# A two-layer recurrent-memory transformer: half-height weight loads and row-paired transposes in the prologue

## The chip, the core and the metric

The kernel runs on one core of a Trainium2 chip. The metric is device time in microseconds for one execution, as the median of several runs. One further execution is profiled; every number of an instruction, an engine or a transfer comes from that one.

## What is computed

Two kinds of layer alternate, twice each, on 2048 tokens of 448 numbers in bf16. The first kind is attention in segments of 32 tokens with a memory of 8 rows that each segment hands to the next, so that the segments of a layer form one chain of 64 steps. The second is a gated feed-forward layer (448 to 1792 and back).

```python
def _A_ref(x, mem0, Wq, Wk, Wv, Wo, seg_len):      # H = 16 heads of Dh = 256
    ...
    for s in range(n_seg):
        xs = x[:, s * seg_len:(s + 1) * seg_len, :].copy()
        h = jnp.concatenate([mem, xs], axis=1)
        q = jnp.einsum('btd,dhe->bhte', h, Wq)
        k = jnp.einsum('btd,dhe->bhte', h, Wk)
        v = jnp.einsum('btd,dhe->bhte', h, Wv)
        scores = jnp.einsum('bhqe,bhke->bhqk', q, k) * scale
        scores = jnp.where(mask[None, None], scores, -1000000000.0)
        p = _softmax(scores, axis=-1)
        o = jnp.einsum('bhqk,bhke->bhqe', p, v)
        o = jnp.einsum('bhte,hed->btd', o, Wo)
        mem = o[:, :M, :].copy()
        outs.append(o[:, M:, :])
    return jnp.concatenate(outs, axis=1)

def _B_ref(x, W_gate, W_up, W_down):
    ...
    h = gate * up                                  # gate with its negative part set to zero
    return jnp.einsum('bsf,fd->bsd', h, W_down)

x = x + _A_ref(_layernorm(x), mem0, Wq, Wk, Wv, Wo, seg_len)
x = x + _B_ref(_layernorm(x), W_gate, W_up, W_down)
x = x + _A_ref(_layernorm(x), mem0, Wq, Wk, Wv, Wo, seg_len)
x = x + _B_ref(_layernorm(x), W_gate, W_up, W_down)
```

## The kernel before

**Two stages.** The kernel does not compute q, k and v. In a prologue it fuses, head by head, Wq with the transpose of Wk into `A_sb` (with `A3`, `A3z` for the last 64 of the 448 dimensions), and Wv with Wo into `B_sb`. The main loop (`step`, from line 830) then takes segment after segment through `A_sb`, the softmax and `B_sb`, with the feed-forward layer (`Feed`) woven in. Both attention layers run in the same steps, the second four steps behind the first. The change is in the prologue alone (lines 100 to 343).

**The prologue's passes.** Two heads are 512 columns of a weight matrix, and 448 rows of it are seven chunks of 64 (`NPASS` = 7). A pass takes one tile `nat` of 128 partitions by 7 by 512, which holds 512 columns of two matrices. There are 12 passes: eight of Wq with Wk (p = 0 to 7), then four of Wv for p and p + 1.

- `load_two` (line 210) loads a pass with four transfers on SP's queue: for each matrix one of 384 rows over all 128 partitions (384 KB) and one of the last 64 rows (64 KB), put into the row half `ROWS[r]` of the middle chunk. `nat` has four buffers. `load_outs` (line 219) loads 512 rows of Wo, 448 KB, after the Wv passes have begun.
- `transposed` (line 230) turns a pass round: four banks of PSUM, `tpw`, one for each 128 of the 512 columns (e), with seven 128 by 128 transposes each, and four copies of 896 elements into `two`, one by ScalarE (ACT) and three by VectorE (DVE). In pass 0 (`first`) the transposes of the first three chunks come before the others, and the copies are shared two and two.
- `fuse_qk` (line 250) multiplies: for three groups of 128 dimensions (kd) and the two heads (eo) products of 384 and of 64 columns, then the last 64 dimensions, with copies by ACT and DVE into `A_sb`, `A3` and `A3z`. `fuse_vo` (line 277) and `fuse_vo_last` do the same for Wv and Wo into `B_sb`.

**The order of PE.** All TensorE (PE) instructions go through `mm` and `tr`, which chain each to the one before (`in_order`), so PE's order is the program's. Transposes of pass p + 1 stand ahead of the products of pass p, but for pass 0, whose products come before the transposes of pass 1:

```python
cur = flip_next(0)
for p in range(NP):
    if p:
        nxt = flip_next(p + 1)
    fuse_qk(p, cur)
    cur = nxt if p else flip_next(1)
```

In the Wv half, the transposes of the next pass stand ahead of the products of two p's. Ahead of it all stand 32 transposes of the identity into `warm` (line 313).

**The other engines and the queues.** The order of DVE, ACT, GpSimd (POOL) and the queue of SP is set by a scheduler that puts ready work first. `tc.keep_in_program_order` (also named `queued`) holds an instruction behind the one traced before it on its engine, without a wait. Weight loads are held so, in the order Wq/Wk passes 0 to 7, Wv 0, Wo 0 and 1, Wv 1, Wo 2 and 3, and so on; three passes are issued at the start, and each `flip_next` asks for one more. Eight semaphores serve the transfers in turn, so that a transfer is issued only when the one eight before it has landed.

**Tokens.** Line 100 loads the first 128 tokens into `xp[1]`, first on SP's queue. Their norm (`row_stats`, `normed`) is written after p = 3, and the transposes of its result after the products of p = 4; the two instructions of `normed` are held in program order, the statistics are not. Lines 340 to 343 and 828 load further tokens into row halves of `xa` and `xp`.

**Constants.** POOL makes the identity, clears `hT` and `TQ` (lines 143 and 155) and copies the mask into `hT`; DVE makes the mask and `blk` (lines 128 and 129).

Of the kernel before, what the change touches and what calls it, by code (L numbers as in the profile page):

```python
# [8 lines left out]
BF = mybir.dt.bfloat16  # L9
F32 = mybir.dt.float32  # L10
# [5 lines left out]
DM = 448  # L16
# [13 lines left out]
TB = BLK * SEG  # L30
# [9 lines left out]
NPASS = 7  # L40
ROWS = (slice(0, 64), slice(64, 128))
# [12 lines left out]
def build_kernel(ctx, tc, A_x, A_mem0, A_Wq, A_Wk, A_Wv, A_Wo, B_W_gate, B_W_up, B_W_down, out,  # L54
                 ntiles=16, nseg=64):
    nc = tc.nc
    P = nc.NUM_PARTITIONS
    x_dram = A_x[0]
# [9 lines left out]
    psum = ctx.enter_context(tc.tile_pool(name="psum", bufs=7, space=bass.MemoryType.PSUM))  # L68
# [12 lines left out]
    def mm(*a, **k):  # L81
        in_order(nc.tensor.matmul(*a, **k))  # L82

    def tr(*a):
        in_order(nc.tensor.transpose(*a))  # L85

    def evac(eng, dst, src):
        if eng is nc.scalar:
            nc.scalar.copy(dst, src)  # L89
        else:  # L90
            eng.tensor_copy(dst, src)  # L91


    xa = [glob.tile([P, DM], BF, name=f"xa{i}") for i in range(3)]
    xp = [glob.tile([P, DM], BF, name=f"xp{i}") for i in range(2)]

    def block(i):
        return slice(TB * i, TB * i + TB)

    nc.sync.dma_start(xp[1][:], x_dram[0:128])  # L100

    ident = glob.tile([P, P], BF, name="ident")
    make_identity(nc, ident[:])

# [8 lines left out]
    rowf = glob.tile([P, 3], F32, name="rowf")  # L113
# [8 lines left out]
    for b in range(4):  # L122
        o = 0 if b % 2 == 0 else MEM
        nc.vector.tensor_scalar(out=maskS[:, b, o:o + SEG], in0=keyf[:, b // 2, :], scalar1=rowf[:, 2:3],
                                scalar2=MASKVAL, op0=ALU.is_gt, op1=ALU.mult)

    blk = glob.tile([P, 2], F32, name="blk")
    nc.vector.tensor_copy(blk[:, 1:2], rowf[:, 1:2])
    nc.vector.tensor_scalar(out=blk[:, 0:1], in0=blk[:, 1:2], scalar1=-1.0, scalar2=1.0,
                            op0=ALU.mult, op1=ALU.add)  # L130

    half = glob.tile([P, 1], F32, name="half")
# [7 lines left out]
    hTb = []  # L140
    for i in range(2):
        t = glob.tile([P, BLK, HW], BF, name=f"hT{i}")
        nc.gpsimd.memset(t[:], 0.0)
        for part, q in enumerate(QR):
            for c in range(2):
                nc.gpsimd.tensor_copy(t[q:q + 16, :, 4 * HI + 64 * c:4 * HI + 64 * c + L],
                                      maskS[q:q + 16, 2 * part + c, :].unsqueeze(1).to_broadcast([16, BLK, L]))
        hTb.append(t)
# [3 lines left out]
    TQ = []  # L152
    for hf in range(2):
        t = glob.tile([P, 5, 6, 64], BF, name=f"TQ{hf}")
        nc.gpsimd.memset(t[:], 0.0)
        TQ.append(t)

    def row_stats(t):

        stats = p_ln.tile([P, nc.vector.BN_STATS_DIM], F32, tag="ln_stats")  # L160
        nc.vector.bn_stats(stats[:], t[:])
        mv = p_ln.tile([P, 2], F32, tag="ln_mv")
        nc.vector.bn_aggr(mv[:], stats[:])
        rstd = p_ln.tile([P, 1], F32, tag="ln_rstd")
        nc.gpsimd.tensor_scalar(out=rstd[:], in0=mv[:, 1:2], scalar1=EPS, scalar2=None, op0=ALU.add)
        nc.gpsimd.tensor_tensor(out=rstd[:], in0=rstd[:], in1=half[:], op=ALU.pow)
        return t, mv, rstd

    def normed(stat):

        t, mv, rstd = stat
        xn = p_ln.tile([P, 512], BF, tag="ln_xn", bufs=3)
        for a, b, o in ((0, DM, 0), (384, DM, DM)):
            tc.keep_in_program_order(
                nc.vector.tensor_scalar(out=xn[:, o:o + b - a], in0=t[:, a:b], scalar1=mv[:, 0:1],  # L175
                                        scalar2=rstd[:], op0=ALU.subtract, op1=ALU.mult))
        return xn
# [24 lines left out]
    with tc.tile_pool(name="pre", bufs=3) as pre:  # L202
# [4 lines left out]

        queued = tc.keep_in_program_order

        def load_two(a, b):  # L210
            t = pre.tile([P, NPASS, 512], BF, tag="nat", name="nat", bufs=4)
            for r, (src, p) in enumerate((a, b)):
                cols = slice(512 * p, 512 * (p + 1))
                queued(nc.sync.dma_start(t[:, 4 * r:4 * r + 3, :],
                                         src[0:384, cols].rearrange("(k p) n -> p k n", p=P)))
                queued(nc.sync.dma_start(t[ROWS[r], 3, :], src[384:448, cols]))
            return t

        def load_outs(p):
# [9 lines left out]

        def transposed(nat, first=False):  # L230
            o = pre.tile([P, 4, 2 * DM], BF, tag="two", name="two", bufs=2)
            tp = [psum.tile([P, 2 * DM], BF, tag="ps", name="tpw") for _ in range(4)]
            order = sorted(((0, i, e) if first and i < 3 else (1, e, i), e, i) for e in range(4) for i in range(NPASS))
            for _, e, i in order:
                tr(tp[e][:, i * 128:(i + 1) * 128], nat[:, i, e * 128:(e + 1) * 128], ident[:])
            for e in range(4):
                evac(nc.scalar if (e % 2 if first else e == 1) else nc.vector, o[:, e, :], tp[e][:])
            return o

        def dims(t, r, e, c, n=1):  # L240
            o = 64 * c if r == 0 else DM + 64 * ((c + 1) % NPASS)
            return t[:, e, o:o + 64 * n]

        def halves(dst, lhs, rhs):
# [5 lines left out]
        def fuse_qk(p, qk):  # L250
            hf, p4 = divmod(p, 4)
            mx_ps = psum.tile([P, 4, 128], F32, tag="ps", name="mxw")
            for kd in range(3):
                for eo in range(2):
                    aps = psum.tile([P, 3, 128], F32, tag="ps", name="aps")
                    for t in range(2):
                        e = 2 * eo + t
                        mm(aps[:, :, :], qk[:, e, kd * 128:kd * 128 + 128], dims(qk, 1, e, 0, 6),
                           start=(t == 0), stop=(t == 1))
                    for t in range(2):  # L260
                        e = 2 * eo + t
                        mm(mx_ps[:, kd, eo * 64:eo * 64 + 64], qk[:, e, kd * 128:kd * 128 + 128], dims(qk, 1, e, 6),
                           start=(t == 0), stop=(t == 1))
                    evac(nc.scalar if eo or kd == 2 else nc.vector,
                         A_sb[:, kd, hf, eo * 4 + p4:eo * 4 + p4 + 17:8, :], aps[:])
            aps = psum.tile([P, 3, 128], F32, tag="ps", name="aps")
            halves(aps, lambda eo, e: qk[:, e, 384:448], lambda e: dims(qk, 1, e, 0, 6))
            for eo in range(2):
                for t in range(2):
                    e = 2 * eo + t  # L270
                    mm(mx_ps[ROWS[hf], 3, eo * 64:eo * 64 + 64], qk[:, e, 384:448], dims(qk, 1, e, 6),
                       start=(t == 0), stop=(t == 1), tile_position=(0, 64 * hf))
            evac(nc.scalar, A3[:, hf, p4:p4 + 9:4, :], aps[:])
            evac(nc.vector, A_sb[:, 0:3, hf, 24 + p4, :], mx_ps[:, 0:3])
            evac(nc.scalar, A3z[ROWS[hf], p4, :], mx_ps[ROWS[hf], 3])
# [20 lines left out]

        def load_next():
            if len(nat) < len(loads):
                nat.append(load_two(*loads[len(nat)]))
            if len(nat) > NP and len(wos) < NP:  # L300
                wos.append(load_outs(len(wos)))
                wos.append(load_outs(len(wos)))

        for _ in range(3):
            load_next()

        def flip_next(i):
            load_next()
            return transposed(nat[i], i == 0)

        warm = psum.tile([P, 2 * DM], BF, tag="ps", name="warm")
        for i in range(32):
            tr(warm[:, 0:128], ident[:], ident[:])
        cur = flip_next(0)
        for p in range(NP):
            if p:
                nxt = flip_next(p + 1)
            fuse_qk(p, cur)
            cur = nxt if p else flip_next(1)
            if p == 3:  # L320
                xn0 = normed(row_stats(xp[1]))
            if p == 4:
                tps0 = transpose_tokens(xn0)
                for b in range(2):
                    rows_in(nc.vector, b, 0, tps0[:, :, block(b)])
                mtp = psum.tile([P, 4, MEM], BF, tag="ps", name="mtp")
                for kd in range(4):
                    tr(mtp[:, kd, :], mem0_n[:, kd * 128:(kd + 1) * 128], ident[0:MEM, 0:MEM])
                nc.vector.tensor_copy(mem0T[:], mtp[:])
                set_mem(0, mem0T[:].unsqueeze(2), (0,))  # L330
# [7 lines left out]

    for i in range(min(3, nblk)):
        nc.gpsimd.memset(xa[i][:], 0.0)  # L340
        nc.sync.dma_start(xa[i][TB:P, :], x_dram[block(i)])
    if nblk > 2:
        nc.sync.dma_start(xp[0][0:TB, :], x_dram[block(2)])


    main = ctx.enter_context(tc.tile_pool(name="main", bufs=1))
# [555 lines left out]
```

## Time and profile before

| | us |
|---|---|
| median of 3 runs | 1600.96 |
| the runs | 1599.98 to 1604.62 |
| profiled execution | 1600.11 |
| its span, first to last instruction | 1598.3 |
| prologue: until the main loop's first weight load | 74.8 |
| transposes of the last Wv pass begin | 62.2 |
| a Wq/Wk pass, from one pass's transposes to the next's | 4.54 |

The span is what lies between the first and the last instruction; 1.8 us of the execution lie around it. Engines are named PE (TensorE products), PEld (its weight loads, which overlap the products), DVE, ACT, POOL and SP. A line of the timeline gives start and duration in us, the engine, the source line, the operation, what it writes and reads, and in brackets how long the engine stood idle before it and what released it; lines of `mm`, `tr` and `evac` are those of the helper (82, 85, 89, 91), so that the tile tells the place. In rows by stretch of time, each engine's busy time is followed by its instruction count, then the granted share of PE's clock, the busy share of the 16 DMA engines (which can be over 1 when packets overlap) and the rate in GB/s.

### The profile page before, as it was taken

What the parts mean: (1) busy time and instruction counts of PE and PEld (TensorE: products, weight loads), DVE (VectorE), ACT (ScalarE), POOL (GpSimd) and SP (SyncE); (2) the same over time, 40 slices, a digit from 0 to 9 for tenths busy, and PEclk for the clock granted to TensorE, in tenths of its full rate; (3) what the DMA queues carried; (4) which work ended last, traced back from release to release, by engine and by line L of the source; (5) the groups of instructions that cost most, each with busy time, mean ns of one, the idle gap of its engine ahead of it and who ended that gap; (6) DMA issues with size and microseconds to landing.
All of it is one profiled execution on the core that took longest, in us unless ns stands there. A gap on an engine that the chain in (4) does not pass through costs nothing.

```text
span 1598.3 us, 96401 instructions
## 1 busy us (share of the span) xinstructions
PE 1567.8 (98%) x44356; PEld 1439.8 (90%) x44356; DVE 1142.5 (71%) x3859; ACT 762.9 (48%) x2239; POOL 92.9 (6%) x240
## 2 busy tenths in 40 slices
PE   8989999999999999999999999999999999999997
PEld 7678899999999999999999999999999999999886
DVE  6856777777777777777777777777777777777773
ACT  5634445544444445544444445544444445544432
POOL 2110000000000000000000000000000000000000
PEclk9989999999999999999999999999999999999999
DMA  9530000000000000000000000000000000000000
GB/s 257 147 102 8 9 9 4 10 9 10 10 10 9 10 10 4 10 10 9 10 10 10 10 10 4 10 10 10 10 9 9 10 10 4 10 8 7 7 7 6
DMA packets 29461, 33.01 MB, mean 21 GB/s; under 512 B 3320, under 2 KB 28160, under 8 KB 29056
## 3 DMA queue, kind: packets, MB, share of 16 engines
q1 hardware_dynamic: 28992, 26.85, 6.3%
q8 instruction: 346, 5.67, 1.5%
q14 instruction: 59, 0.48, 0.1%
q0 software_dynamic: 64, 0.01, 0.0%
HBM read 23.18 MB, written 1.84 MB: 16 GB/s over the span
## 4 chain that ended last, share of the span: by engine, by line
PE 89%; DVE 7%; ACT 1%; POOL 1%; issue 1%; DMA 0%; POOLq 0%; ACTq 0%; DVEq 0%
PE prj L82 25%; PE ox L82 25%; PE ups L82 10%; PE dps L82 6%; PE o L82 5%; PE y L82 4%; PE Sx L82 2%; PE Sm L82 2%; PE bps L82 1%; PE tpw L85 1%; DVE xn L175 1%; DVE TQ L91 1%; PE aps L82 1%; PE gps L82 1%; PE tps L85 1%; PE pps L85 1%
## 5 line engine op out<-in xcount | busy, mean ns | idle before, releaser
L82 PEld LDWEIGHTS <-B_sb 128*128 128x128 bf16 (+1 forms) x15456 | 495.0, 103 | 27.7 <-issue 19.9
L82 PE MATMUL prj<-hT,A_sb 128*128 128x80 bf16 (+1 forms) x11424 | 441.7, 200 | 0.4 <-issue 0.4
L82 PEld LDWEIGHTS <-A_sb 128*128 128x128 bf16 x11424 | 411.9, 100 | 8.9 <-issue 0.5
L82 PE MATMUL ox<-Y,B_sb 128*128 128x80 bf16 (+4 forms) x5880 | 223.0, 198 | 1.8 <-DVE Y L636 1.8
L82 PE MATMUL ox<-Z,B_sb 128*128 128x80 bf16 (+2 forms) x5712 | 217.7, 199 | 1.3 <-DVE Z L636 1.3
L89 ACT CAST TQ<-prj 128x480 bf16<-128x480 f32 (+1 forms) x380 | 178.5, 497 | 83.0 <-PE prj L82 58.7
L82 PE MATMUL gps<-xT,Wgu_sb 64*128 64x128 bf16 (+1 forms) x3332 | 191.3, 214 | 0.8 <-issue 0.5
L82 PE MATMUL ups<-xT,Wgu_sb 64*128 64x128 bf16 (+1 forms) x3332 | 191.1, 214 | 1.0 <-DVE xT L416 0.5
L82 PEld LDWEIGHTS <-Wgu_sb 64*128 64x128 bf16 x6664 | 179.4, 95 | 4.8 <-issue 2.5
L91 DVE CAST TQ<-prj 128x480 bf16<-128x480 f32 (+1 forms) x228 | 129.3, 573 | 13.4 <-PE prj L82 11.2
L432 DVE SCALAR_TENSOR_TENSOR hh<-gps,ut 128x256 bf16<-128x256 f32 (+1 forms) x238 | 95.3, 407 | 48.0 <-ACT ut L431 35.3
L431 ACT CAST ut<-ups 128x256 bf16<-128x256 f32 (+1 forms) x238 | 85.4, 359 | 83.4 <-PE gps L82 64.9
L91 DVE CAST Y<-y 64x128 bf16<-64x128 f32 (+2 forms) x256 | 102.2, 420 | 14.4 <-ACT Y L89 4.5
L89 ACT CAST Y<-y 64x128 bf16<-64x128 f32 (+2 forms) x256 | 89.4, 379 | 46.6 <-DVE Y L91 41.5
L91 DVE CAST Z<-y 64x128 bf16<-64x128 f32 (+2 forms) x256 | 99.2, 418 | 12.4 <-ACT Z L89 5.5
L89 ACT COPY hT<-tps 128x256 bf16<-128x256 bf16 x32 | 11.9, 372 | 197.5 <-DVE hT L91 197.5
L563 DVE COPY PT<-pps 128x128 bf16<-128x128 bf16 (+1 forms) x206 | 49.6, 254 | 79.1 <-PE pps L85 77.5
L545 ACT ACTIVATE se<-se 128x80 f32<-128x80 f32 (+1 forms) x270 | 71.4, 298 | 68.0 <-DVE se L544 67.2
L89 ACT CAST TZ<-prj 64x320 bf16<-64x320 f32 (+2 forms) x152 | 56.2, 380 | 98.8 <-DVE TZ L91 94.0
L89 ACT CAST Z<-y 64x128 bf16<-64x128 f32 (+2 forms) x256 | 89.2, 378 | 23.9 <-DVE Z L91 17.4
L82 PEld LDWEIGHTS <-hk 40*128 40x128 bf16 (+1 forms) x1989 | 79.9, 95 | 20.5 <-issue 10.6
L551 DVE TENSOR_REDUCE ssum<-se 128x2 f32<-128x80 f32 (+1 forms) x270 | 70.8, 274 | 35.9 <-ACT se L545 33.6
(128 smaller groups left out, 2254.6 us busy)
## 6 DMA issues: line engine op xcount, KB each, us to landing
wo<-in_A_Wo_dram SPq DMA_DIRECT2D x8, 448.0 KB, 7.6
nat<-in_A_Wq_dram SPq DMA_DIRECT2D x8, 384.0 KB, 5.5
nat<-in_A_Wk_dram SPq DMA_DIRECT2D x8, 384.0 KB, 6.1
nat<-in_A_Wv_dram SPq DMA_DIRECT2D x8, 384.0 KB, 7.6
xa<-in_A_x_dram SPq DMA_DIRECT2D x32, 56.0 KB, 2.4
xa<-xp SPq DMA_DIRECT2D x32, 56.0 KB, 1.9
out_dram<-xa SPq DMA_DIRECT2D x32, 56.0 KB, 2.0
xp<-in_A_x_dram SPq DMA_DIRECT2D x30, 56.0 KB, 2.3
```

The lines of the kernel that those rows point to most:

```text
L82: in_order(nc.tensor.matmul(*a, **k))
L85: in_order(nc.tensor.transpose(*a))
L89: nc.scalar.copy(dst, src)
L91: eng.tensor_copy(dst, src)
L175: nc.vector.tensor_scalar(out=xn[:, o:o + b - a], in0=t[:, a:b], scalar1=mv[:, 0:1], scalar2=rstd[:], op0=ALU.subtract, op1=ALU.mult))
L431: nc.scalar.copy(ut[:, :, n], ups[:, :, n])
L432: nc.vector.scalar_tensor_tensor(out=hh[:, 2 * u:2 * u + 2, n], in0=gps[:, :, n], scalar=0.0, in1=ut[:, :, n], op0=ALU.max, op1=ALU.mult)
L545: nc.scalar.activation(se[:], se[:], AF.Exp, scale=SCALE)
L551: nc.vector.tensor_reduce(ssum[:], se[:], axis=AX.X, op=ALU.add)
L563: nc.vector.tensor_copy(PT[:], pps[:].rearrange("p b q -> p (b q)"))
```

## The change

- **Loads.** A pass is loaded with two transfers of 448 KB instead of four: the matrix of r = 0 goes to partitions 0 to 63 and that of r = 1 to partitions 64 to 127, seven chunks of 64 rows each. In pass 0 each matrix comes in two halves of 256 columns (512 bytes in a row), Wq on SP's queue and Wk on ACT's.
- **Transposes.** Each transposes 64 rows by 128 columns; the two row halves of `nat` go into two banks, one after the other for the same columns. Two banks are filled and copied at a time (e = 0, 1 and then 2, 3). A copy takes one matrix and two e's (896 elements), in pass 0 one e (448 elements, shared by DVE and ACT). `dims` follows the new layout.
- **Products of pass 0** run eo = 0 for all three kd first and then eo = 1; the other passes keep their order.
- **Fillers.** The identity transposes ahead of pass 0 become 24 instead of 32, and ten more stand between the transposes of pass 0 and its products.
- **Tokens.** The first 128 tokens are loaded behind the first three passes; their statistics are held in program order on DVE; the later token loads are held on SP behind all weight loads.
- **POOL and DVE.** `blk` is made by POOL; the clearings of `hT` and `TQ` are held in program order.

```diff
-    nc.sync.dma_start(xp[1][:], x_dram[0:128])
...
-    nc.vector.tensor_copy(blk[:, 1:2], rowf[:, 1:2])
-    nc.vector.tensor_scalar(out=blk[:, 0:1], in0=blk[:, 1:2], scalar1=-1.0, scalar2=1.0,
+    nc.gpsimd.tensor_copy(blk[:, 1:2], rowf[:, 1:2])
+    nc.gpsimd.tensor_scalar(out=blk[:, 0:1], in0=blk[:, 1:2], scalar1=-1.0, scalar2=1.0,
                             op0=ALU.mult, op1=ALU.add)
...
-        nc.gpsimd.memset(t[:], 0.0)
+        tc.keep_in_program_order(nc.gpsimd.memset(t[:], 0.0))
...
-    def row_stats(t):
+    def row_stats(t, pin=False):
...
-        nc.vector.bn_stats(stats[:], t[:])
+        (tc.keep_in_program_order if pin else lambda i: i)(nc.vector.bn_stats(stats[:], t[:]))
...
-        def load_two(a, b):
+        def load_two(a, b, first=False):
             t = pre.tile([P, NPASS, 512], BF, tag="nat", name="nat", bufs=4)
-            for r, (src, p) in enumerate((a, b)):
-                cols = slice(512 * p, 512 * (p + 1))
-                queued(nc.sync.dma_start(t[:, 4 * r:4 * r + 3, :],
-                                         src[0:384, cols].rearrange("(k p) n -> p k n", p=P)))
-                queued(nc.sync.dma_start(t[ROWS[r], 3, :], src[384:448, cols]))
+            n = 256 if first else 512
+            for o in range(0, 512, n):
+                for r, (src, p) in enumerate((a, b)):
+                    eng = nc.scalar if first and r else nc.sync
+                    queued(eng.dma_start(t[ROWS[r], :, o:o + n],
+                                         src[:, 512 * p + o:512 * p + o + n].rearrange("(c p) n -> p c n", p=64)))
             return t
...
             o = pre.tile([P, 4, 2 * DM], BF, tag="two", name="two", bufs=2)
-            tp = [psum.tile([P, 2 * DM], BF, tag="ps", name="tpw") for _ in range(4)]
-            order = sorted(((0, i, e) if first and i < 3 else (1, e, i), e, i) for e in range(4) for i in range(NPASS))
-            for _, e, i in order:
-                tr(tp[e][:, i * 128:(i + 1) * 128], nat[:, i, e * 128:(e + 1) * 128], ident[:])
-            for e in range(4):
-                evac(nc.scalar if (e % 2 if first else e == 1) else nc.vector, o[:, e, :], tp[e][:])
+            for ep in range(2):
+                tp = [psum.tile([P, 2, DM], BF, tag="ps", name="tpw") for _ in range(2)]
+                for k in range(2):
+                    for i in range(NPASS):
+                        for r in range(2):
+                            e = 2 * ep + k
+                            tr(tp[r][:, k, 64 * i:64 * i + 64], nat[ROWS[r], i, e * 128:(e + 1) * 128], ident[ROWS[r], ROWS[r]])
+                for k in range(2) if first else (slice(0, 2),):
+                    for r in range(2):
+                        es = slice(2 * ep + k, 2 * ep + k + 1) if first else slice(2 * ep, 2 * ep + 2)
+                        evac(nc.scalar if r and (first or ep == 0) else nc.vector,
+                             o[:, es, DM * r:DM * r + DM], tp[r][:, k:k + 1, :] if first else tp[r][:])
             return o
...
-            o = 64 * c if r == 0 else DM + 64 * ((c + 1) % NPASS)
+            o = DM * r + 64 * c
...
-            for kd in range(3):
-                for eo in range(2):
+            for kd, eo in [(kd, eo) for eo in range(2) for kd in range(3)] if p == 0 else \
+                    [(kd, eo) for kd in range(3) for eo in range(2)]:
...
-                nat.append(load_two(*loads[len(nat)]))
+                nat.append(load_two(*loads[len(nat)], first=not nat))
...
+        queued(nc.sync.dma_start(xp[1][:], x_dram[0:128]))
...
-        for i in range(32):
-            tr(warm[:, 0:128], ident[:], ident[:])
+        def idle(n):
+            for _ in range(n):
+                tr(warm[:, 0:128], ident[:], ident[:])
+
+        idle(24)
         cur = flip_next(0)
+        idle(10)
...
-                xn0 = normed(row_stats(xp[1]))
+                xn0 = normed(row_stats(xp[1], True))
...
-        nc.sync.dma_start(xa[i][TB:P, :], x_dram[block(i)])
+        tc.keep_in_program_order(nc.sync.dma_start(xa[i][TB:P, :], x_dram[block(i)]))
     if nblk > 2:
-        nc.sync.dma_start(xp[0][0:TB, :], x_dram[block(2)])
+        tc.keep_in_program_order(nc.sync.dma_start(xp[0][0:TB, :], x_dram[block(2)]))
```

More of the change, by code (lines that the diff above doesn't have):

```diff
@@ L154, in build_kernel @@
         t = glob.tile([P, 5, 6, 64], BF, name=f"TQ{hf}")
-        nc.gpsimd.memset(t[:], 0.0)
+        tc.keep_in_program_order(nc.gpsimd.memset(t[:], 0.0))
         TQ.append(t)
-    def row_stats(t):
+    def row_stats(t, pin=False):
         stats = p_ln.tile([P, nc.vector.BN_STATS_DIM], F32, tag="ln_stats")
-        nc.vector.bn_stats(stats[:], t[:])
+        (tc.keep_in_program_order if pin else lambda i: i)(nc.vector.bn_stats(stats[:], t[:]))
         mv = p_ln.tile([P, 2], F32, tag="ln_mv")
@@ L252, in fuse_qk @@
             mx_ps = psum.tile([P, 4, 128], F32, tag="ps", name="mxw")
-            for kd in range(3):
-                for eo in range(2):
[L255 to L265, printed above, removed]
+            for kd, eo in [(kd, eo) for eo in range(2) for kd in range(3)] if p == 0 else \
+                    [(kd, eo) for kd in range(3) for eo in range(2)]:
+                aps = psum.tile([P, 3, 128], F32, tag="ps", name="aps")
+                for t in range(2):
+                    e = 2 * eo + t
+                    mm(aps[:, :, :], qk[:, e, kd * 128:kd * 128 + 128], dims(qk, 1, e, 0, 6),
+                       start=(t == 0), stop=(t == 1))
+                for t in range(2):
+                    e = 2 * eo + t
+                    mm(mx_ps[:, kd, eo * 64:eo * 64 + 64], qk[:, e, kd * 128:kd * 128 + 128], dims(qk, 1, e, 6),
+                       start=(t == 0), stop=(t == 1))
+                evac(nc.scalar if eo or kd == 2 else nc.vector,
+                     A_sb[:, kd, hf, eo * 4 + p4:eo * 4 + p4 + 17:8, :], aps[:])
             aps = psum.tile([P, 3, 128], F32, tag="ps", name="aps")
```

## The prediction

> **What bounds the kernel now.** I read first the page's busy rows and the chain that ended last, then stretches of the first 100 us, then the timeline, because the change touches only the prologue (up to 74.8 us) and the transfers behind it.
>
> ```profile
> span 1598.3 us, 96401 instructions
> PE 1567.8 (98%) x44356; PEld 1439.8 (90%) x44356; DVE 1142.5 (71%) x3859; ACT 762.9 (48%) x2239; POOL 92.9 (6%) x240
> PE 89%; DVE 7%; ACT 1%; POOL 1%; issue 1%; DMA 0%; POOLq 0%; ACTq 0%; DVEq 0%
> ```
>
> PE sets the end almost everywhere; DMA has no share of the chain. In stretches (time, then PE, PEld, DVE, ACT, POOL busy, granted clock, DMA share, GB/s):
>
> ```profile
> 5.00:10.00 5.00, 3.23 (x34) 2.26 (x31) 1.15 (x2) 1.71 (x2) 4.86 (x9) 1.00 0.94 281
> 10.00:15.00 5.00, 3.29 (x42) 2.58 (x43) 2.78 (x6) 2.33 (x6) 2.92 (x7) 1.00 1.12 290
> 15.00:20.00 5.00, 5.00 (x73) 4.12 (x71) 4.08 (x8) 3.43 (x7) 0.00 (x0) 1.00 1.03 260
> 25.00:30.00 5.00, 5.00 (x72) 4.03 (x70) 3.72 (x7) 3.65 (x8) 0.00 (x0) 1.00 0.92 257
> 45.00:50.00 5.00, 5.00 (x67) 3.84 (x65) 3.72 (x8) 3.80 (x8) 0.00 (x0) 1.00 1.09 319
> ```
>
> The reader sees PE waiting only before 15 us and full after it, while the transfers keep ahead. The timeline (start, duration, engine, line) gives the waits and the price of a pass:
>
> ```profile
> 7.59 1.05 PE L85 MATMUL tpw<-ident,nat 128*128 128x128 bf16 x16 [1.31 <-DMA nat<-in_A_Wk_dram]
> 12.20 0.93 DVE L175 TENSOR_SCALAR xn<-xp,mv,rstd 128x448 bf16<-128x448 bf16 x1 [3.02 <-POOL rstd L166]
> 13.63 0.52 PE L82 MATMUL aps<-two 128*64 128x384 bf16 x4 [1.70 <-DVE A_sb L91]
> 24.81 1.57 PEld L85 LDWEIGHTS <-nat 128*128 128x128 bf16 x28
> 25.47 1.88 DVE L91 COPY two<-tpw 128x896 bf16<-128x896 bf16 x3
> 29.35 1.57 PEld L85 LDWEIGHTS <-nat 128*128 128x128 bf16 x28
> 62.19 1.56 PEld L85 LDWEIGHTS <-nat 128*128 128x128 bf16 x28 [0.36 <-issue]
> 74.80 0.21 PEld L82 LDWEIGHTS <-A 64*128 64x128 bf16 x12 [0.36 <-DVE B_sb L91]
> ```
>
> A Wq/Wk pass lasts 29.35 - 24.81 = 4.54 us, 1.57 of it transposes. Pass 0 is late: it waits for Wk until 7.59 and for DVE, which sits behind the token norm (L175), until 13.63; the next transposes begin at 14.18. From the last transposes (62.19) to the main loop (74.80) are 12.6 us.
>
> **The change part by part.**
>
> Row pairs. 28 transposes become 28 pairs of 64-row ones with 64 moving columns. The nearest row is the gate/up product of the same shape, two row halves into two banks:
>
> ```profile
> 137.14 1.28 PEld L82 LDWEIGHTS <-Wgu_sb 64*128 64x128 bf16 x84
> ```
>
> (1.28 - 0.10)/83 = 14.3 ns each, 28.6 ns a pair; 28 pairs are 0.80 us, with the last one's 0.1 us left over some 0.84, against 1.57. That saves 0.73 us in each of 11 passes, 8.0 us of PE. Bounds: nothing saved (no overlap) to 0.77. The copies stay four of 896 elements, three on DVE and one on ACT. Per pass DVE then has 1.88 + 1.01 + 0.56 = 3.45 us and ACT 0.91 + 0.48 + 1.25 + 0.48 + 0.26 = 3.38, in a pass that would last 4.54 - 0.73 = 3.81: tight, but not the bound.
>
> The start. Tokens (112 KB) no longer lead the queue, pass 0 comes in halves on two queues, and bn_stats is held back. Before, all of Wk was in at 7.5 us; less 112 KB at the 281 GB/s of that stretch (0.4) it is 7.1, and up to 6.2 if two queues at once fill the engines as the later stretches (319) do. I take 6.8; the first half some 2.1 us sooner. Packets of 512 bytes appear nowhere in the trace; if they cost as much as the 1 KB ones, pass 0 takes 2.6 us more, if half as much, nothing; the linear guess from the 896-byte packets puts them near half. ACT issues two transfers at about 0.6 us each (SP's rows say 0.37 to 0.59); ACT is idle until 8.24 now, so this costs nothing, and would cost 1.2 us in the first copy without that cover. Second half transposed by 7.5, ten filler transposes 0.6 (54 ns each) to 8.1, the first products with eo = 0 and eo = 1 1.1 us each (0.38 per kd in the rows of pass 1), then 0.5: pass 0 ends near 10.8 instead of 14.18. Gain 3.4.
>
> Token norm at pass 3. bn_stats, bn_aggr (0.63 + 0.18), the POOL pair (0.23 + 0.57 and hand-overs, some 1.0), two norms (0.93 + 0.29): 3.1 us of DVE in order, with the copies of the next pass queued behind. Before it cost PE 1.70. It may cost 0 (hidden where PE waits for transfers anyway) to 2.5 (3.1 less DVE's slack of some 0.4 and a little more). The two blk operations (0.14 + 0.15) go to POOL, which idles until 35.8 in the trace. The memsets held on POOL stand in that order already. The five later x loads move from 16-19 us, where they sit between Wq loads, behind the last Wo load; xa is first read at 129 us, so nothing. SP issues 2 instead of 4 a pass: 1.1 us of SP saved that nothing waits for; but eight transfers outstanding now span four passes instead of two.
>
> Loads on one row half. This is the term that decides. A pass is 2 x 448 KB = 917.5 KB. Three bounds from rows: full-width loads keep 319 to 324 GB/s. Wgu's loads alternate between the halves exactly so. The five x loads of 19 to 21 us, each on one half, three in a row on the same one, are the floor:
>
> ```profile
> 19.00:20.00 1.00, 1.00 (x13) 0.69 (x11) 0.24 (x1) 1.00 (x3) 0.00 (x0) 1.00 0.73 127
> 20.00:21.00 1.00, 1.00 (x21) 0.91 (x18) 0.62 (x2) 0.74 (x3) 0.00 (x0) 1.00 0.60 152
> 79.00:81.00 2.00, 2.00 (x80) 1.88 (x73) 1.27 (x8) 1.51 (x8) 1.90 (x5) 1.00 1.00 253
> 81.00:83.00 2.00, 1.10 (x25) 0.87 (x24) 1.54 (x8) 0.53 (x3) 2.00 (x2) 1.00 1.01 240
> 36.00:55.00 19.00, 19.00 (x215) 13.29 (x212) 14.46 (x26) 13.81 (x29) 0.09 (x1) 1.00 1.10 324
> ```
>
> I take 245 GB/s (Wgu, the nearest shape, DMA share 1.0, so saturated): X = 917.5/245 = 3.74 us a load, ends at 3.06 (300) and 6.1 (151). The last Wv pair lands at 6.8 + 0.4 (tokens behind pass 2) + 11 X + 3 x 2.83 (two Wo per group at 324) = 15.7 + 11 X = 56.8. After it come its transposes, 0.84, and the last four fuse_vo: 12.6 - 1.56 = 11.0, so 11.9 in all. End of prologue 27.6 + 11 X = **68.7**. The path of PE alone is shorter: 10.8 + 0.84 + 7 x 3.81 + 3 x 0.84 + 4 x 5.5 (56.7 to 62.2) = 62.8, or 65.3 with the norm's 2.5. So transfers become the bound, and PE waits some 0.3 us a pass and longer in the Wv groups.
>
> Behind the prologue everything (Wgu loads, POOL's Y and Z memsets) is released by its last products and moves along. Sum: 68.7 - 74.8 = -6.1 us. The profiled execution took 1600.11 us (span 1598.3 and 1.8 around it), so 1594.0; the median of the runs is 0.85 above it: **1594.9 us**.
>
> The clock adds noise: after PE's wait at 82-84 us the granted clock is 0.77 in 80-90 and 0.55 in 90-100. A shift of the prologue may cut or lengthen this; +-2 us.
>
> **The rivals.**
>
> PE sets the pace (22%). If the two halves interleave over the 16 engines as well as full rows do, X = 3.06 and transfers would end at 61.3; PE's 62.8 to 65.3 counts: 1588.1 to 1590.6 on the profiled run, about 1590.2 as a median. For it: pass 0's first Wgu loads ran at 294 GB/s in 77-78. Against: they fall to 240 once the queue is full.
>
> Halves overlap only partly (18%). If the engines stay mostly in step on one half, the rate lies between the x loads' 152 and Wgu's 245, say 199: X = 4.6, end 78.2, +3.4, about 1604. For it: a nat load keeps each engine on a half for 28 packets, Wgu for 4. The Trainium skill, "SBUF — State Buffer", section "Can I just issue two DMAs to hit both halves?", speaks against the change: two transfers on the two halves gained only 6% over one, 196 GB/s in its table; by that, an estimate of 208 GB/s and 4.4 us a load, the time would be about 1602. By that rule the Wgu rows should not exceed it; they show 240 to 253, so the trace agrees only in direction.
>
> In lockstep, slower (10%). All engines on one half at a time, at the x loads' 151 GB/s: X = 6.1, end 94.7, +20, 1621. The sign turns at X = 4.29 (214 GB/s); it is 0.3% slower from 4.73 (194). Against it: the sixteen engines' shares of one Wgu load land over some 2 us, longer than the load itself takes at 245, so they do not march in step.
>
> Pairs don't overlap (5%). Transposes stay 1.57 and PE's path is 62.8 + 8 = 70.8 to 73.3; -1.5 to -4: 1597 to 1599.5. Against it: the gate/up row.
>
> **How the numbers follow.** The forecast has 45%, its own range 1591.5 to 1598.5 (X from 3.44 to 4.05). This kernel's runs differ by 0.3% (4.8 us) without cause, so faster means X under 3.86, 238 GB/s. Faster: 0.22 and two thirds of 0.45, 0.52; same: the rest of the forecast, the pairs, most of the partly overlapped, 0.35; slower: 0.13. Range 1588 to 1604.5: it leaves out the lockstep and the best edge.
>
> **What would show it.** Transposes: 28 pairs in some 0.8 us. GB/s near 245 with DMA share 1.0 between 10 and 35 us, PE waiting for nat, pass period near 3.8. Transposes after pass 0 near 11 us, last Wv transposes near 57, main loop's first weights near 68.7. Wrong: a pass period of 4.3 or more, or PE without waits for nat.

## The result, and the profile after

The change makes the kernel slower: 1615.40 us (median of 4 runs, 1613.00 to 1617.62) against 1600.51 (median of 4, 1599.98 to 1604.62), a ratio of 1.0084 [1.0071, 1.0098]. The profiled execution of the changed kernel is the slowest of its four, 1617.62 us, 17.5 above that of the kernel before. One execution of a version below, the profiled one of even_odd (2129.89 us), ran at a granted clock of 0.75 throughout; its time is left out there.

The busy rows and the shares of the chain that ended last, changed kernel:

```profile
span 1615.8 us, 97051 instructions
PE 1570.6 (97%) x44694; PEld 1435.9 (89%) x44694; DVE 1141.0 (71%) x3859; ACT 763.7 (47%) x2241; POOL 93.5 (6%) x242
PE 88%; DVE 7%; issue 2%; ACT 1%; DMA 1%; POOL 1%; SPq 0%; ACTq 0%; POOLq 0%; DVEq 0%
```

Two shares of the chain are larger than before: DMA went from 0% to 1%, and "issue", time in which an engine waited for nothing that the profile shows, from 1% to 2%. One per cent of the span is 16 us, about the size of the loss; the shares are rounded, so they only say where to look. In stretches of 5 us of the changed kernel (columns as above: PE, PEld, DVE, ACT, POOL busy, granted clock, DMA share, GB/s):

```profile
20.00:25.00 5.00, 4.12 (x92) 2.99 (x90) 3.21 (x8) 3.37 (x7) 0.00 (x0) 1.00 1.13 209
35.00:40.00 5.00, 3.11 (x32) 1.89 (x32) 1.97 (x5) 0.48 (x1) 0.00 (x0) 0.50 1.12 210
50.00:55.00 5.00, 2.14 (x41) 1.50 (x40) 1.61 (x4) 2.06 (x6) 0.00 (x0) 1.00 1.12 245
```

The 16 DMA engines are full (share 1.12 to 1.13). They move 209 and 210 GB/s, and 245 from 50 us, where Wo's full-height loads stand among the others; before they moved 257 and 319 (25 to 30 and 45 to 50 us), with PE full. Now PE is full in none of the three, and in the second its clock is halved as well. The timeline of the changed kernel says what it waits for:

```profile
5.79 0.77 PEld L85 LDWEIGHTS <-nat 64*128 64x128 bf16 x28 [1.90 <-DMA nat<-in_A_Wq_dram]
10.02 0.85 PE L82 MATMUL aps<-two 128*128 128x384 bf16 x2
18.23 0.87 PEld L85 LDWEIGHTS <-nat 64*128 64x128 bf16 x55 [2.30 <-DMA nat<-in_A_Wk_dram]
34.60 0.61 DVE L173 TENSOR_SCALAR xn<-xp,mv,rstd 128x448 bf16<-128x448 bf16 x2 [1.01 <-POOL rstd L164]
36.89 0.53 PEld L85 LDWEIGHTS <-nat 64*128 64x128 bf16 x18 [4.06 <-issue]
37.59 1.16 DVE L91 COPY two<-tpw 128x896 bf16<-128x896 bf16 x2 [2.38 <-PE tpw L85]
55.86 1.12 PE L85 MATMUL tpw<-ident,nat 64*128 64x64 bf16 x35 [3.72 <-issue]
64.80 6.32 PE L82 MATMUL bps<-wo,two 128*128 128x448 bf16 x27 [2.06 <-issue]
89.46 0.21 PEld L82 LDWEIGHTS <-A 64*128 64x128 bf16 x12 [0.36 <-DVE B_sb L91]
```

There are two kinds of wait. Up to 23 us PE waits for `nat`, as the transfers are late. Behind that the long waits, 4.06 us at 32.83 to 36.89, then 3.84 and 2.31 as weight loads count them (3.72 and 2.06 in the products' rows), stand in the middle of a run of like instructions: at 36.89, 37 of a pass's 56 row transposes are through, and 19 follow. DVE is not in the way at 36.89: it waited itself, for PE. Counted along PE's records (weight loads and products), the waits fall on the 705th, 961st, 1217th, 1473rd and 1729th, 256 apart. Just ahead of each of the four longest the records of the transfers show one 16 KB packet of the queue "instruction" (ends at 35.46, 44.63, 54.23 and 63.28 us); PE goes on 1.4 to 1.6 us behind it. The page's row of that queue:

```profile
q8 instruction: 349, 5.72, 1.5%
```

349 packets of 256 instructions are 89344, and PE's products and weight loads together 89388: this queue brings PE's instructions. The reading is that PE has run out of them; lean and two_bufs below test it. The five waits of this kind are 0.68 + 4.06 + 0.97 + 3.84 + 2.31 = 11.9 us. The time from PE's step into a block of 256 to the first packet of the fetch that follows is called the fetch's wait below. It is 5.9 to 7.3 us from 18 us on, against 2.3 to 2.4 in the kernel before (blocks from 32.84 and 42.38 us).

The main loop's first weights come at 89.46 instead of 74.80 us: 14.66 us of the 17.5. The other 2.8 lie behind the prologue. Between the medians lie 14.9 us, and the profiled execution is the slowest of the four, so that the 2.8 may be its own; the others have no profile.

What stood outstanding shows in the page's rows of DMA issues (last column: median us from issue to landing), first of the kernel before:

```profile
nat<-in_A_Wq_dram SPq DMA_DIRECT2D x8, 384.0 KB, 5.5
```

and of the changed one:

```profile
nat<-in_A_Wq_dram SPq DMA_DIRECT2D x7, 448.0 KB, 13.9
```

### The profile page after: what moved, and what is told of

It is laid out like the page before. It is cut to its first block, busy times and chain, and to the rows that moved or that the text cites. A ratio compares the mean times of both kernels' runs of the same rounds, so it can differ in the third digit from the quotient of the medians.

```text
span 1615.8 us, 97051 instructions
## 1 busy us (share of the span) xinstructions
PE 1570.6 (97%) x44694; PEld 1435.9 (89%) x44694; DVE 1141.0 (71%) x3859; ACT 763.7 (47%) x2241; POOL 93.5 (6%) x242
## 4 chain that ended last, share of the span: by engine, by line
PE 88%; DVE 7%; issue 2%; ACT 1%; DMA 1%; POOL 1%; SPq 0%; ACTq 0%; POOLq 0%; DVEq 0%
PE prj L82 25%; PE ox L82 25%; PE ups L82 10%; PE dps L82 6%; PE o L82 5%; PE y L82 4%; PE Sx L82 2%; PE Sm L82 2%; PE bps L82 1%; DVE TQ L91 1%; PE aps L82 1%; DVE xn L173 1%; PE gps L82 1%; PE tps L85 1%; PE pps L85 1%
## 5 line engine op out<-in xcount | busy, mean ns | idle before, releaser
L89 ACT COPY hT<-tps 128x256 bf16<-128x256 bf16 x32 | 11.9, 372 | 198.2 <-DVE hT L91 179.0
L82 PE MATMUL dps<-Wd_sb,hh 128*128 128x448 bf16 x476 | 96.9, 355 | 0.0
## 6 DMA issues: line engine op xcount, KB each, us to landing
wo<-in_A_Wo_dram SPq DMA_DIRECT2D x8, 448.0 KB, 13.2
nat<-in_A_Wk_dram SPq DMA_DIRECT2D x7, 448.0 KB, 14.5
```

## The experiments

Two theories stood first: the loads on one partition half cost it all, by their rate and by what they do to the fetch; or the row pairs cost it, by using up PE's instructions faster. All edits are against the changed kernel. "Full-height loads" are those of the kernel before. Times with an interval are ratios to the kernel before on the same chip.

**full_pairs: full-height loads, all else as changed.** The copies put the 64-row pieces where the old layout has them.

```diff
-                    queued(eng.dma_start(t[ROWS[r], :, o:o + n],
-                                         src[:, 512 * p + o:512 * p + o + n].rearrange("(c p) n -> p c n", p=64)))
+                queued(nc.sync.dma_start(t[:, 4 * r:4 * r + 3, :],
+                                         src[0:384, cols].rearrange("(k p) n -> p k n", p=P)))
+                queued(nc.sync.dma_start(t[ROWS[r], 3, :], src[384:448, cols]))
```

> The changed kernel with the loads of before (384 rows over 128 partitions and 64 rows on a half, four transfers a pass, pass 0 too), row-paired transposes kept; the copies put the chunks in order. Theory A, the half-height transfers are to blame (209 GB/s, and PE's instruction fetches wait behind them): 290 GB/s or more between 20 and 50 us, no PE gap over 1 us after pass 0, main loop begins at 63 to 67 us, 1589 to 1594 us. Rival B, the pairs are to blame because they double PE's instructions and PE waits for its 256-instruction blocks: gaps of 2 to 4 us at every 256 instructions stay (some 12 us), main loop at 75 to 80 us, 1601 to 1606 us.

1595.93 us against 1602.37, 0.9965 [0.9951, 0.9979]: faster. The main loop starts at 69.01 us. Start and time lie past the 63 to 67 and 1589 to 1594 us that were expected if the loads cost it all, and short of the 75 to 80 and 1601 to 1606 expected if the pairs do. Its stretches, and the one long wait of PE behind pass 1, from the timeline:

```profile
20.00:25.00 5.00, 5.00 (x101) 3.58 (x100) 4.28 (x9) 4.08 (x10) 0.00 (x0) 1.00 1.09 292
35.00:40.00 5.00, 5.00 (x135) 3.83 (x134) 3.63 (x8) 4.32 (x10) 0.00 (x0) 1.00 1.10 319
```

```profile
29.73 0.48 PE L82 MATMUL aps<-two 128*128 128x384 bf16 x2 [1.31 <-DVE two L91]
```

PE is full, the rate is 291 to 321 GB/s from 5 to 50 us, a 1 KB packet takes 58 ns on average (10 to 50 us) instead of 87, and the fetch waits 2.1 to 4.5 us. One gap is left at a block's end (1.05 us at 44.78) and one of 1.40 us that is the token norm's.

**half_singles: half-height loads, but whole 128-row transposes** (the copies sort the rows).

```diff
-                            tr(tp[r][:, k, 64 * i:64 * i + 64], nat[ROWS[r], i, e * 128:(e + 1) * 128], ident[ROWS[r], ROWS[r]])
...
+                    tr(tp[e][:, i * 128:(i + 1) * 128], nat[:, i, e * 128:(e + 1) * 128], ident[:])
...
+                evac(nc.scalar if (e % 2 if first else e == 1) else nc.vector,
+                     o[:, e, :].rearrange("p (r i q) -> p r i q", r=2, q=64),
+                     tp[e][:].rearrange("p (i r q) -> p i r q", r=2, q=64))
```

> The changed kernel with its half-height loads, but 28 transposes of 128 rows a pass as before (the copies sort the columns). Theory A: loads still at 205 to 215 GB/s, the last Wv pair lands near 72 us, main loop near 84 us, 1608 to 1612 us; fetch gaps small, since 120 PE instructions per 4.6 us need a block only every 9.8 us. Rival B: without the doubled instructions the loss is gone, main loop near 75 us, about 1600 us.

1610.50 us, 1.0061 [1.0043, 1.0079]; main loop at 83.52. One stretch, and the longest of four waits from the timeline:

```profile
30.00:35.00 5.00, 5.00 (x68) 3.90 (x67) 3.73 (x9) 3.37 (x8) 0.43 (x2) 1.00 1.12 206
```

```profile
54.16 3.06 PE L85 MATMUL tpw<-ident,nat 128*128 128x128 bf16 x28 [2.79 <-DMA nat<-in_A_Wv_dram]
```

The rate is that of the changed kernel, so the pairs have no part in it. PE waits for `nat` four times (2.38, 1.77, 2.90 and 1.30 us from 14 us on) and never at a block's end, although the fetch waits 4.0 to 5.9 us up to 50 us here: a pass has 120 PE instructions instead of 176, a block lasts some 9.6 us instead of the 5.5 to 6 that row pairs without a stall would make it, and covers the fetch.

**full_singles: loads and transposes of the kernel before**, so that only the start, the tokens, the fillers and pass 0's order remain of the change.

```diff
+            order = sorted(((0, i, e) if first and i < 3 else (1, e, i), e, i) for e in range(4) for i in range(NPASS))
+            for _, e, i in order:
+                tr(tp[e][:, i * 128:(i + 1) * 128], nat[:, i, e * 128:(e + 1) * 128], ident[:])
```

> Loads and transposes as before; only the rest of the change stays (token load and its statistics later, 24 and 10 fillers, eo first in pass 0, POOL's share, later token loads last). Theory A: the start gains what the token norm cost, 1 to 2 us, and the norm costs part of it at pass 3: main loop at 73 to 75 us, 1598.5 to 1601 us. Rival C, the new order of the start or the late norm costs several us: main loop after 77 us, over 1603 us.

1600.90 us, 0.9997 [0.9984, 1.0010]; main loop at 73.20. With it the starts of the main loop (us) form a square:

| | 128-row transposes | row pairs |
|---|---|---|
| full-height loads | 73.20 | 69.01 |
| half-height loads | 83.52 | 89.46 |

Pairs alone bring 4.2 us, half-height loads alone cost 10.3; together they should stand at 79.3 and stand at 89.5. The 10.2 between has two parts. With half-height loads the transfers set the end, whatever the transposes cost: half_singles starts its main loop 12.65 us after the last Wv pass landed (70.87), and that is the 11.9 from there to the end with 0.73 for whole transposes. So the pairs' 4.2 can't be had there. The other 5.9 are 89.46 less 83.5, and two_bufs below, with pairs and half-height loads but without the stalls, starts at 83.97: the pairs ask for instructions faster, the loads deliver them later.

**half_fine: the half-height transfers cut in two**, the two matrices' pieces in turn.

```diff
-            for o in range(0, 512, n):
+            for o, c0, c1 in [(0, 0, 7), (256, 0, 7)] if first else [(0, 0, 4), (0, 4, 7)]:
```

> The changed kernel, each later load cut into chunks 0 to 3 and 4 to 6, alternating between the row halves (16 or 12 packets per engine on a half instead of 28). If the loss comes from engines staying in step on one half for long, as the forecast put it, the rate rises from 209 towards the 245 GB/s of the feed-forward loads, main loop at 80 to 84 us, 1605 to 1610 us. If a half-height transfer is slow however short it is, 205 to 215 GB/s and 1613 to 1618 us stay.

1611.87 us, 1.0057 [1.0034, 1.0080]: the time falls between the two expectations, the start of the main loop within the first:

```profile
82.30 0.21 PEld L82 LDWEIGHTS <-A 64*128 64x128 bf16 x12 [0.36 <-DVE B_sb L91]
```

That is 7.2 us sooner than in the changed kernel. The last Wv pass lands at 67.84 instead of 71.66, and PE ends 2.6 us behind the transfers' bound (11.9 after that landing) instead of 5.9. The rate in the stretches of 10 to 35 us is 216 to 220 GB/s, where it was 201 to 213; nothing like the 245 of Wgu's loads. From issue to landing are 8.5 to 10.0 us instead of 13 to 14.5, the fetch waits 4.7 to 5.8, and the gaps at the block ends are 2.20 + 0.90 + 2.47 + 1.72 = 7.3 us instead of 11.9. The first of them in the timeline:

```profile
33.88 0.69 PE L85 MATMUL tpw<-ident,nat 64*128 64x64 bf16 x19 [2.11 <-issue]
```

**even_odd and even_odd2: 64 rows to a transfer, but on the even or the odd partitions** (half_singles otherwise).

```diff
-                    queued(eng.dma_start(t[ROWS[r], :, o:o + n],
+                    queued(eng.dma_start(t[r:P:2, :, o:o + n],
```

> Half-height transfers again, 64 partitions each with the same seven chunks, the same two transfers a pass and 128-row transposes, but the first matrix goes to the even partitions and the second to the odd ones (the copies sort the columns). If what slows a transfer is that it lies in one half of the partitions, whatever its rows and count: 290 GB/s or more between 20 and 35 us, 1 KB packets at 58 instead of 88 ns, main loop at 73 to 76 us, 1598 to 1603 us. If it is the shape (64 rows of seven chunks, two long transfers): 205 GB/s, 88 ns, main loop at 83 to 84 us, 1609 to 1612 us, as with one matrix per half and 128-row transposes.

1604.61 us (median of nine) against 1602.31, 1.0008 [0.9995, 1.0021], a little past the 1598 to 1603 expected and far from 1609. The same kernel once more, for a second profile (one run, 1600.79 us against 1600.44):

> The same kernel as in the run with one matrix on the even and the other on the odd partitions, for a second profile. If what is slow is that a transfer lies within one half of the partitions, the loads run at 290 GB/s or more with 1 KB packets of 55 to 60 ns, and the main loop starts at 73 to 76 us as with full-height loads. If what is slow is that a transfer has 64 rows to a chunk, whichever partitions these are, the rate is 200 to 215 GB/s, packets take 86 to 90 ns, and the main loop starts at 82 to 84 us.

```profile
5.00:10.00 5.00, 4.84 (x43) 4.25 (x42) 2.18 (x2) 1.81 (x2) 4.72 (x11) 1.00 1.03 332
10.00:15.00 5.00, 5.00 (x67) 3.87 (x65) 3.07 (x5) 3.27 (x7) 2.15 (x3) 1.00 1.10 350
```

The same bytes, rows and transfers run at 332 to 350 GB/s up to 20 us, a 1 KB packet in 52 ns on average (10 to 50 us). It is the partition half that is slow, not the 64 rows. The main loop starts at 76.35, a little past the range: DVE is full from 15 to 30 us, since its copies gather single numbers with a stride, and that takes the gain.

**lean: fewer bytes under the same PE program.** Passes after the fourth load three of seven chunks; those parts of the weights are left out.

```diff
+            nc_ = NPASS if seen[0] < 4 else 3
...
-                    queued(eng.dma_start(t[ROWS[r], :, o:o + n],
-                                         src[:, 512 * p + o:512 * p + o + n].rearrange("(c p) n -> p c n", p=64)))
+                    queued(eng.dma_start(t[ROWS[r], 0:nc_, o:o + n],
+                                         src[0:64 * nc_, 512 * p + o:512 * p + o + n].rearrange("(c p) n -> p c n", p=64)))
```

> The changed kernel, but the transfers of the passes after the fourth bring only three of the seven chunks (the other four chunks keep what an earlier pass left there, so those parts of the weights are left out of the computation). PE's instruction stream is the same, instruction for instruction, and the transfers still lie on one partition half, but they come to 43% of the bytes and no longer fill the engines. If the wait of PE's instruction fetch (5.9 to 7.0 us in the changed kernel) comes from standing behind saturated half-height loads, the wait falls to some 2.5 us, the gaps at every 256th PE instruction vanish behind about 30 us, and the main loop starts at 66 to 71 us. If it comes from PE's own greater number of instructions (the rival: 176 in a pass instead of 120, one block of 256 every 5.5 to 6 us), the waits stay near 6 us with gaps of 2 to 4 us after 50 us, and the main loop starts at 75 us or later.

The waits on PE from 25 us to the main loop, all that are over 0.25 us:

```profile
34.98 0.48 PE L82 MATMUL aps<-two 128*128 128x384 bf16 x2 [1.31 <-DVE two L91]
50.98 4.63 PE L82 MATMUL bps<-wo,two 128*128 128x448 bf16 x27 [0.31 <-issue]
```

The first is the token norm's; of the waits at block ends one is left, 0.57 us on the weight loads. The fetch's packets come 0 to 3.3 us after PE's step into a block from 26 us on, and 5.5 after it at 18.68, while the whole-size loads still ran. PE runs through its blocks faster than in the changed kernel (a Wq/Wk pass every 3.9 us), so its appetite for instructions is not the cause by itself; the full transfers ahead of the fetch are. The main loop starts at 73.95, outside the 66 to 71 expected: the first four passes have their whole size, and PE waited 1.72 + 1.51 + 2.92 + 1.06 = 7.2 us for them up to 23 us, against 2.35 in full_pairs. That 4.9 is the distance to 69.01. (One run, 1601.53 us against 1600.44, says nothing on the time.)

**two_bufs: two buffers of `nat` instead of four**, so that fewer transfers are outstanding.

```diff
-            t = pre.tile([P, NPASS, 512], BF, tag="nat", name="nat", bufs=4)
+            t = pre.tile([P, NPASS, 512], BF, tag="nat", name="nat", bufs=2)
```

> The changed kernel with two buffers for a pass's weights instead of four, so that fewer transfers stand outstanding (in the changed kernel a load lands 13.9 to 14.5 us after its issue, in the kernel before 5.5 to 6.1). If the instruction fetch of PE waits because it stands behind the outstanding half-height transfers, the time from issue to landing falls to 7 to 10 us, the fetch wait falls from 5.9 to 7.0 us to 3 to 4.5, and the gaps at every 256th PE instruction, 11.9 us in the changed kernel, fall under 5 us; loads may then start late, so the main loop starts at 84 to 90 us. If the wait does not depend on what is outstanding (the rival: each packet of the fetch is simply slow while half-height writes go on), it stays at 6 to 7 us, the gaps stay at 10 us or more, and the main loop starts at 89 to 95 us.

```profile
nat<-in_A_Wq_dram SPq DMA_DIRECT2D x7, 448.0 KB, 6.4
```

```profile
52.01 0.20 PE L85 MATMUL tpw<-ident,nat 64*128 64x64 bf16 x1 [1.45 <-DMA nat<-in_A_Wv_dram]
54.27 1.67 PE L85 MATMUL tpw<-ident,nat 64*128 64x64 bf16 x55 [2.06 <-DMA nat<-in_A_Wv_dram]
72.01 0.99 PE L85 MATMUL tpw<-ident,nat 64*128 64x64 bf16 x55 [1.97 <-DMA nat<-in_A_Wv_dram]
```

No wait of 0.4 us or more at a block's end is left: 11.9 us became none. In the Wq/Wk passes, which now land 6.4 to 7.4 us after their issue, the fetch's first packet comes 0.1 to 3.0 us after PE's step into a block, less than the 3 to 4.5 expected. In the Wv passes, where transfers still take 11.8 us, it comes after 5.6 and 4.3 us, under blocks of 10.8 and 14.5 us that cover it. PE's waits of 0.4 us and more behind 14 us all end with a landing of `nat`, and the main loop starts at 83.97, at the edge of the 84 to 90 expected, that is 11.96 after PE got the last Wv pass (72.01): the bound of the transfers alone. One run gave 1611.45 us against 1601.73. So the fetch's wait depends on the transfers that are outstanding; with four buffers and half-height loads these were up to eight.

**norm_split and best: the useful part.** norm_split is full_pairs with the token statistics one pass ahead of the norm:

```diff
+            if p == 2:
+                st0 = row_stats(xp[1], True)
             if p == 3:
-                xn0 = normed(row_stats(xp[1], True))
+                xn0 = normed(st0)
```

> The changed kernel with the loads of before, row pairs kept; the token statistics now after the products of p = 2, the norm after those of p = 3, so that DVE doesn't wait for POOL's root. If the 1.4 us that PE waits there come from DVE waiting 1.0 us for POOL: the wait goes, main loop at 67.6 to 68.2 us instead of 69.0. If they come from DVE's own work (two norms, statistics): unchanged.

1594.49 us against 1602.31, 0.9951 [0.9938, 0.9963]: the fastest version, better than both kernels. The gap of 1.40 us at the norm is gone and the main loop starts at 68.1; two gaps at block ends are there (0.70 us at 14.34 and 1.18 at 43.74). By time alone it can't be told from full_pairs; the intervals overlap. best adds the kernel before's order for pass 0 (first three chunks first), with 24 of the fillers between:

```diff
+            if first:
+                turn(0, range(3))
+                turn(1, range(3))
+                idle(24)
```

> As the one with split norm; in pass 0 the pairs of the three chunks that arrive first come first, with 24 fillers before the rest, instead of 10 after all. Expected if pass 0 is held by the late second matrix and by the clock that falls to half after PE's wait of 2.35 us: no half clock before 12 us, pass 0 done 1 to 2 us sooner, main loop at 66 to 67 us, 1592 to 1595 us. If the transposes are not what holds pass 0: no gain.

1596.57 us, 0.9963 [0.9950, 0.9977]. Pass 1's transposes begin 1.2 us sooner (11.6 instead of 12.8), and all of it is given back: PE waits at 12.62 (1.09 us, pass 2 has not landed), 14.12, 20.69 and 44.14, and the main loop starts at 70.21, not at the 66 to 67 expected. The last three waits, 0.92 + 1.10 + 1.88 = 3.9 us, stand at block ends; the longest:

```profile
46.02 0.20 PEld L85 LDWEIGHTS <-nat 64*128 64x128 bf16 x10 [1.88 <-issue]
```

So with row pairs the fetch costs something under full-height loads too.

## Why the prediction was wrong

**The step that failed first is the load of a pass, X = 917.5 KB / 245 GB/s = 3.74 us.** It measured 4.60: from the landing of pass 0 (8.07) to that of the first Wv pass (45.43) are eight loads, less 0.55 for the tokens (112 KB at this rate). That is 199 GB/s over the stretch, 201 to 213 by the windows. The Wgu rows were the wrong stand-in: there each matrix is cut so that an engine stays on a half for 4 packets, here for 28. half_fine, with 16 and 12, gained some 5% in the rate of these passes (X = 4.46 by the same sum), and a group of Wv with two Wo took 7.9 us instead of 8.7, so the length of a stay can be a small part of it; what else lets Wgu's loads run at 240 to 253 was not tried. The prediction had the right value among its rivals ("Halves overlap only partly", X = 4.6, about 1604), at 18%. The Trainium skill, "SBUF — State Buffer", section "Can I just issue two DMAs to hit both halves?", from which 208 GB/s was estimated, came within the measured 201 to 213; the trace bears it out for these loads, and it was given too little weight.

**The time is 11 us over that rival too**, since three more terms of the sum were off. Against the forecast's 68.7 us for the start of the main loop, 89.46 is 20.8 more:

| term | forecast | measured | us |
|---|---|---|---|
| a load X, 11 times | 3.74 | 4.60 | +9.5 |
| pass 0 landed | 6.8 | 8.07 | +1.3 |
| two Wo beside a half-height load | 2.83 (324 GB/s) | 4.14 | +3.9 |
| PE behind the transfers' bound | 0 | 5.9 | +5.9 |

The third comes from the landings of the four Wv passes, 45.43 to 71.66: a group takes 8.74 us, less 4.60 for its own load, so it holds what that load costs there over 4.60 as well. The last is 89.46 less 71.66 and 11.9; two_bufs, with the same loads and no stall at a block's end, ends on that bound. The terms make 20.6 of the 20.8.

**The last term was not in the sum at all.** PE's instruction fetch was named nowhere in the prediction; the row it would have had to look at, PE's waits at every 256th instruction, shows nothing in the kernel before, because the fetch's wait of 2.3 us is hidden under a block of 9.5. The change shortened the cover to 5.5 to 6 us and lengthened the wait to 5.9 to 7.3. Alone, the longer wait cost nothing at block ends (half_singles) and the shorter cover 1.1 to 3.9 us (full_pairs, norm_split, best). Of the 11.9 us of stalls 5.9 show in the end, as the others lie where PE would have waited for transfers. The halved clock that stands around these stalls (34.7 to 41.6, 55.2 to 58.6 and 65.4 to 68.9 us) is in the 5.9 as well; two_bufs, without stalls at block ends, has one such stretch behind 25 us (53.1 to 60.0), where its longest wait for `nat` is. The Trainium skill, "Runtime: NRT & Kernel Launch", section "Instruction fetch mechanics", says that instructions come in blocks of 16 KiB, 256 of them, and that crossing one is mostly hidden. The 256 and the 16 KB agree with this trace; the hiding holds for the kernel before and fails here.

**Row pairs: right.** 56 row transposes took 0.87 to 0.90 us where 0.84 was forecast and 28 whole ones 1.57. Alone they bring 4.2 us of the 8.0 counted; full_pairs has waits of PE for transfers, for the norm and for one fetch (2.35, 1.40 and 1.05 us) that can account for the rest.

**The start: wrong in two places, harmless in size.** Pass 0 landed at 8.07, not 6.8, as the half-height rate was already there (202 GB/s in 5 to 10 us; in even_odd2 the same pieces, their rows also 512 bytes long, landed at 6.49); and its products took 5.0 us instead of 2.7: a pair 0.83 to 0.85 us instead of 0.49. That is what a pair takes from 37 to 41 us too, where the granted clock is 0.50. The trace has no entry of the clock before 14.25 us, and at that point the pairs fall back, so a halved clock is likely here and not shown. So pass 1's transposes began at 15.04, later than the 14.18 before, instead of 10.8 forecast. It is off the path here, since pass 2 lands at 18.2 anyway. With full-height loads the whole start is worth 1.6 us (full_singles, 74.80 to 73.20).

**The norm: within its range.** 0 to 2.5 us was allowed; 1.40 in full_pairs, of which POOL's two instructions are 1.01 of DVE's wait; norm_split shows that it can be had for nothing.

**The chances.** "Slower" had 0.13, and the range ended at 1604.5. The sign hung on X alone, and the measured 199 GB/s lies within its bounds (151 to 300); the value between them was read from the row alike in alternating halves, and not in size. The lower bound said little: in its stretch the engines' share was 0.60, so 152 GB/s was not the rate of full engines.

## What to carry to other kernels

A load that writes 64 partitions of one half cost here as if it had half again the bytes (87 to 89 against 58 ns a packet); alternating the halves in the queue did not make it good, so save TensorE work (row pairs paid here) by sorting in the copies, not by the layout of the load. When PE gets more and shorter instructions, compare the time of 256 of them with the time of an instruction fetch under the transfers of that stretch: a wait put down to "issue" in the middle of a run of like instructions, at every 256th, points to that fetch. Deep prefetch was not free: with half-height loads, half the buffers removed every such stall.

## What the runs showed of the hardware

- Over 10 to 50 us a 1 KB packet on one partition half took 87 to 89 ns on average (changed kernel, half_singles), 58 in full-height loads (full_pairs), and 52 in transfers of 64 rows on every second partition (even_odd2). The rates of the weight passes with full engines were 201 to 213, 291 to 321 and 332 to 350 GB/s.
- The packets of PE's instruction fetch stand in the records of the same 16 DMA engines as the weights, and the fetch's wait was longer where those took longer from issue to landing (medians): 2.3 us with 5.5 to 7.6 (kernel before), 0.1 to 3.0 with 6.4 to 7.4 (two_bufs, Wq/Wk), 4.7 to 5.8 with 8.5 to 10.4 (half_fine), 5.9 to 7.3 with 13.2 to 14.5 (changed kernel). That is not all of it: half_singles has 4.0 to 5.9 with 12.9 to 14.6. The engines were full at times in all five (share up to 1.09 to 1.16), so their busy share does not tell it. By which order the engines serve the queues no run shows.
